# An attention and MoE kernel: dummy matmuls moved to another PSUM bank, six more hidden blocks split into high and low parts, and a scheduler's priorities shifted in 21 stretches

## The chip, the cores and the metric

The kernel runs on one core of one Trainium2 chip. The metric is the device time of one execution in microseconds (us), the median of three runs. Engines are called as in the profile: PE is TensorE, PEld its weight loads, DVE is VectorE, ACT is ScalarE, POOL is GpSimd, SP is SyncE, which issues most DMAs.

## What is computed

Three layers follow each other on 4 batches of 1088 tokens. The attention has 4 heads of 32; its features are products of two projections with 8 columns each.

```python
def phi(x):
    a = einsum('rd,bhsd->bhsr', S1, x)
    b = einsum('rd,bhsd->bhsr', S2, x)
    return einsum('bhsi,bhsj->bhsij', a, b).reshape(*x.shape[:-1], r * r)
kv, z = einsum('bhsf,bhsd->bhfd', phi(k), v), phi(k).sum(axis=2)
x = einsum('bhsf,bhfd->bhsd', phi(q), kv) / (einsum('bhsf,bhf->bhs', phi(q), z)[..., None] + 1e-6)

# x goes on as [4, 1088, 128]
x_prev = x shifted by one token
xk = mu_k * x + (1 - mu_k) * x_prev
xr = mu_r * x + (1 - mu_r) * x_prev
k = maximum(xk @ w_k, 0)                      # 1024 hidden columns
x = sigmoid(xr @ w_r) * ((k * k) @ w_v)

h = maximum(x @ w_in, 0)                      # 1024 columns, halves u and v
v_n = (v - mean(v)) / sqrt(var(v) + 1e-6)
v_s = einsum('ts,bsd->btd', w_spatial, v_n) + b_spatial[None, :, None]
out = (u * v_s) @ w_out
```

## The kernel before

Tokens of a batch are cut into chunks of 384, 384 and 320 (CH), so there are 12 chunks. The hidden columns are cut into blocks of 128: 8 blocks a chunk, 96 blocks in all, numbered g.

Most f32 matmuls are made from fp32r parts: mm3 (line 402) adds three products, low times high, high times high and high times low; the high part is a rounded copy made by ACT (line 405), the low part a subtraction (low, line 408) on DVE or POOL. Each block g goes up (up: three matmuls, relu on ACT at line 679), is squared (sqsplit), and goes down 4 blocks later (down). The letters of PAT say how a block is squared: 'D' squares on ACT (line 700) and goes down as one plain f32 matmul (line 724, two rows of the profile); 'S' multiplies on DVE (line 688), copies the high part on ACT, takes the low part on DVE, and goes down by mm3; 'Q' is as 'S', but its square lies in SBUF and its low part is taken on POOL. G1 and G2 say from which g each pattern holds: the third pattern from g = 26 to 71.

Weights arrive as 64-bit words. split64 (lines 415 to 425) turns them into a high and a low part by five steps on DVE, two or three on ACT, and for 512 columns a product on POOL (line 423). In the start these conversions share DVE with the attention of the first chunks: features (line 521) makes the 64 products per head, k_sum sums keys with values, k_blocks (line 551) masks the sum, q_turn transposes the query features (line 573, into banks 6 and 7) and ACT copies them out, q_num multiplies (line 481) and divides (lines 595 to 597), q_out transposes back (line 611), prep mixes two tokens (lines 617, 636 and 639) and splits the result. Matmuls of a "visit" use half of the array (64 by 64 tiles, line 481) and are kept together.

Dummy matmuls on zeros stand at the start (10 at line 1160) and wherever PE has nothing else to do (keep_busy, line 497, first 8 and then 40); all write bank 7.

No order is written out by hand. The program is recorded first, and arrange then places every instruction: it keeps a planned time for each engine, and among the instructions that could start soon it takes the one with the lowest rank, which is its place in the recorded program. Dummies have a rank behind everything. The result is fixed: each engine runs its list in that order. depend tells arrange which instruction waits for which.

Of the kernel before, what the change touches and what calls it, by code (L numbers as in the profile page):

```python
# [35 lines left out]
IW = 256  # L36
# [18 lines left out]
V2 = 3  # L55
PAT = ('D', 'SD', 'SD', 'S', 'S')
UT = 'x0'
# [34 lines left out]
MARGIN = (30000, 2500)  # L92
IDLE = (8, 40)
SOON = 100
SLACK = {"PE": 60, "Activation": 150, "DVE": 150, "Pool": 200, "SP": 0}
RATES = ((3300, 200), (5000, 300), (8000, 280), (10600, 215), (24000, 350), (float("inf"), 340))
# [103 lines left out]
def depend(todo):  # L200
# [3 lines left out]
    for k, i in enumerate(todo):  # L204
        w, e = {}, engine_name(i)
        for t, (lo, hi, m), write in accesses(i):
# [12 lines left out]
            if t.name.startswith("p"):  # L219
                for k2, lo2, hi2, *_ in seen[name]:  # L220
                    e2 = engine_name(todo[k2])
                    if k2 != k and (e == e2 == "PE" or e != e2 and lo < hi2 and lo2 < hi):
                        w[k2] = w.get(k2, False) or e != e2
# [9 lines left out]
def arrange(tc, after, chain, idle, soon):  # L233
# [33 lines left out]
    lanes = []  # L267
    rank = list(range(len(todo)))
    for k in reversed(range(len(todo))):
# [86 lines left out]
def attn_moe_gmlp(ctx: ExitStack, tc: tile.TileContext, qT, kT, va, st, wk, wv, wr, win, wout,  # L356
# [14 lines left out]
    def bank(i):  # L371
        uid[0] += 1
        return pp.tile([128, 512], F32, tag=f"p{i}", bufs=1, name=f"p{i}_{uid[0]}")
# [120 lines left out]
    def keep_busy(n):  # L494
        w = bank(7)[:, :IW]
        for x in range(n):
            idle.add(TE.matmul(w, lhsT=zero[:, :128], rhs=zero, start=x == 0, stop=x == n - 1).ins.name)  # L497
# [63 lines left out]

    def q_feat(i, wide):
        qp = qst[i] = sb("n1L", [128, 3, 256])
        return features(q_s[i // 3], i % 3, qp, wide, GE if i in QP else None)
# [15 lines left out]

    def q_num(i):
        b, c = divmod(i, 3)
        qt, kb = qst[i], kbd[b]
        nd = bank(5)[:, :396].rearrange("p (t h c) -> p t h c", t=3, h=NH)
        for t in range(3):
# [426 lines left out]
    def group(b, p):  # L1012
# [114 lines left out]
        if last_group:  # L1127
            while gout:
                flush()
            ob = sb(rot(m(6), m(7)), [128, CMAX])  # L1130
            for h in range(2):
                cs = slice(CMAX // 2 * h, CMAX // 2 * h + CMAX // 2)
                tt(VE, u2[:, cs], Z[:, cs], u2[:, cs], ALU.add)
                VE.scalar_tensor_tensor(out=u2[:, cs], in0=pu[:, cs], scalar=0.0, in1=u2[:, cs], op0=ALU.max, op1=ALU.mult)
                TE.matmul(po[1][:, cs], lhsT=wo_last, rhs=u2[:, cs], start=False, stop=h == 1)
            copy(ob, po[1])
            nc.sync.dma_start(out=out[:, b * S + CMAX:b * S + 2 * CMAX], in_=ob)
        else:
            flush()
            pu = pre(d, 1)  # L1140
            gated_out(pu, join(Z, u2), d, 1)
# [15 lines left out]
    VE.memset(zero.bitcast(F32), 0.0)  # L1157
    wp = bank(7)[:, :IW]
    for n in range(NWARM):
# [89 lines left out]

    NI = B * NCH  # L1250
    def meet(sums, num, feat, key):
        wide = bank(4) if (sums, feat, key) != (None,) * 3 else None
        steps = []
        if sums is not None:
            steps.append((k_sums, sums, wide[:, 384:]))
        if num is not None:
            steps.append((q_num, num))
        if feat is not None:
            steps.append((q_feat, feat, wide[:, :192]))
        if key is not None:  # L1260
            steps.append((k_feat, *key, wide[:, 192:384]))
        visit(*steps)

    for g, *what in MEET:
        plan(g, gated(meet) if g < 3 else meet, *what)
    FQ = {f: g for g, _, _, f, _ in MEET if f}
    for j in range(1, NI):
        num = next(g for g, _, n, _, _ in MEET if n == j)
        e = num + OUT
# [206 lines left out]
```

## Time and profile before

| | |
|---|---|
| median of three runs | 438.68 us (438.68 to 438.85) |
| profiled execution | 438.73 us |
| its span, first to last instruction | 436.5 us |
| PE busy | 430.1 us, 3169 matmuls |
| DVE busy | 312.7 us |
| ACT busy | 269.8 us |
| POOL busy | 178.7 us |
| granted PE clock, share of full | 1.00 |

The profile comes from one execution on the chip. Times in its rows count from the start of the span; the execution lasts 2.23 us longer than the span. The start of a row is the start of its first instruction, and PE's rows overlap, because matmuls are pipelined: how fast PE goes is read from one row's start to the next.

### The profile page before, as it was taken

The page shows a single profiled execution, that of the slowest core. Times are in us where ns is not written, and L with a number is a line of the kernel's source. Part 1 is how long each engine was busy: PE and PEld are TensorE (multiplying, and loading weights), DVE is VectorE, ACT ScalarE, POOL GpSimd, SP SyncE. Part 2 cuts the span into 40 slices and gives each one's busy share as a digit, 9 for nine tenths or more (in the row PEclk, how much of TensorE's full clock was granted, in tenths as well). Part 3 has the DMA queues.
Part 4 walks back from the last instruction along what each step waited for, and adds up shares of the span by engine and source line. Part 5 has one row for each costly group of instructions (what it writes and reads, how often), then busy time and mean ns, then how long its engine had stood idle before and what let it go on. Part 6 is the DMA issues. An engine that isn't in the chain of part 4 may idle for free.

```text
span 436.5 us, 8536 instructions
## 1 busy us (share of the span) xinstructions
PE 430.1 (99%) x3169; PEld 402.2 (92%) x3169; DVE 312.7 (72%) x596; ACT 269.8 (62%) x631; POOL 178.7 (41%) x222
## 2 busy tenths in 40 slices
PE   8999999999999999999999999999999999999996
PEld 7968898888888999999999999999999999999995
DVE  5899999889988998684569987834757834525314
ACT  2797999998988987653447654434544434443331
POOL 4153456534345622513321466545346625334220
PEclk9999999999999999999999999999999999999999
DMA  7965010121011111322365223222113222100001
GB/s 228 365 210 177 0 54 20 37 56 47 2 47 32 34 36 38 112 82 73 112 216 176 63 75 119 76 72 65 60 50 119 74 73 65 61 9 16 2 2 50
DMA packets 31385, 34.98 MB, mean 80 GB/s; under 512 B 2864, under 2 KB 26864, under 8 KB 31344
## 3 DMA queue, kind: packets, MB, share of 16 engines
q1 hardware_dynamic: 31056, 34.36, 25.0%
q8 instruction: 25, 0.41, 0.4%
q14 instruction: 16, 0.13, 0.1%
q10 hardware_dynamic: 288, 0.08, 0.1%
HBM read 25.91 MB, written 8.52 MB: 79 GB/s over the span
## 4 chain that ended last, share of the span: by engine, by line
PE 82%; DVE 11%; ACT 3%; POOL 2%; issue 1%; POOLq 0%; DVEq 0%; ACTq 0%
PE p L402 63%; PE p L481 6%; PE p L724 6%; DVE VR L822 3%; PE p L573 2%; DVE bn L816 1%; DVE m L939 1%; PE p L1040 1%; PE p L1039 1%; DVE m L408 1%; POOL rs L819 1%; PE p L611 1%; PE p L497 1%; DVE VR L939 1%; PE p L1160 1%
## 5 line engine op out<-in xcount | busy, mean ns | idle before, releaser
L402 PE MATMUL p<-m,k 128*128 128x384 f32 (+1 forms) x288 | 69.5, 357 | 0.3 <-DVE w L408 0.2
L402 PE MATMUL p<-w,k 128*128 128x384 f32 (+1 forms) x360 | 63.4, 323 | 0.0
L402 PEld LDWEIGHTS p<-w,k 128*128 128x128 f32 x360 | 58.9, 188 | 0.7
L939 DVE TENSOR_TENSOR m<-p,m 128x384 f32<-128x384 f32 (+2 forms) x37 | 19.2, 518 | 55.5 <-PE p L1040 54.9
L402 PEld LDWEIGHTS p<-m,k 128*128 128x128 f32 x288 | 48.0, 188 | 9.1 <-DVE w L408 2.2
L405 ACT ACTIVATE m<-m 128x384 fp32r<-128x384 f32 (+2 forms) x46 | 23.3, 506 | 46.1 <-DVE m L1053 35.4
L408 POOL TENSOR_TENSOR k<-VR,k 128x512 fp32r<-128x512 f32 x25 | 33.0, 1319 | 41.1 <-ACT k L405 36.7
L679 ACT ACTIVATE m<-p 128x384 f32<-128x384 f32 (+1 forms) x96 | 44.8, 473 | 4.1 <-PE p L402 3.6
L405 ACT ACTIVATE m<-p 128x384 f32<-128x384 f32 (+2 forms) x44 | 20.8, 476 | 33.4 <-PE p L402 24.9
L408 DVE TENSOR_TENSOR m<-m,m 128x384 fp32r<-128x384 f32 (+1 forms) x44 | 30.7, 697 | 11.0 <-ACT m L405 10.4
L402 PE MATMUL p<-w,n1H 128*128 128x384 f32 (+1 forms) x192 | 37.5, 325 | 0.0
L402 PE MATMUL p<-w,n1L 128*128 128x384 f32 (+1 forms) x168 | 33.1, 323 | 0.0
L408 POOL TENSOR_TENSOR w<-st,w 128x384 fp32r<-128x384 f32 (+1 forms) x15 | 14.9, 995 | 43.5 <-ACT w L405 43.4
L688 DVE TENSOR_TENSOR p<-p,m 128x384 f32<-128x384 f32 (+1 forms) x56 | 29.6, 533 | 4.0 <-ACT m L679 3.4
L402 PEld LDWEIGHTS p<-w,n1H 128*128 128x128 f32 x192 | 32.0, 188 | 0.4
L822 DVE TENSOR_SCALAR VR<-VR,mv,rs 128x512 f32<-128x512 f32 x24 | 22.0, 915 | 12.6 <-POOL rs L819 12.5
L405 ACT ACTIVATE k<-VR 128x512 fp32r<-128x512 f32 x25 | 15.8, 631 | 21.4 <-PE p L402 16.5
L402 PEld LDWEIGHTS p<-w,n1L 128*128 128x128 f32 x168 | 28.2, 188 | 0.3
L724 PE MATMUL p<-w,wvT 128*128 128x384 f32 (+1 forms) x72 | 28.0, 470 | 0.0
L818 POOL TENSOR_SCALAR rs<-mv 128x1 f32<-128x1 f32 x34 | 9.6, 282 | 44.9 <-DVE mv L817 44.2
L408 DVE TENSOR_TENSOR w<-p,w 128x384 fp32r<-128x384 f32 (+1 forms) x48 | 25.2, 532 | 1.9 <-ACT w L405 1.5
L408 POOL TENSOR_TENSOR n1H<-VR,n1H 128x512 fp32r<-128x512 f32 x12 | 16.5, 1373 | 23.8 <-ACT n1H L405 23.6
(279 smaller groups left out, 1147.0 us busy)
## 6 DMA issues: line engine op xcount, KB each, us to landing
vd<-VR SPq DMA_DIRECT2D x24, 256.0 KB, 2.0
VR<-vd SPq DMA_DIRECT2D x24, 256.0 KB, 2.8
st<-in_wT_dram SPq DMA_DIRECT2D x16, 192.0 KB, 2.4
w<-in_kT_dram SPq DMA_DIRECT2D x8, 192.0 KB, 4.5
w<-in_qT_dram SPq DMA_DIRECT2D x8, 192.0 KB, 3.5
VR<-in_wT_dram SPq DMA_DIRECT2D x8, 192.0 KB, 2.4
out_dram<-m SPq DMA_DIRECT2D x8, 192.0 KB, 1.9
m<-in_wT_dram SPq DMA_DIRECT2D x8, 192.0 KB, 3.0
```

Of the source, the lines that this page charges most:

```text
L402: TE.matmul(out_ap, lhsT=l, rhs=r, start=first and n == 0, stop=last and n == 2, skip_group_check=skip)
L405: return SE.activation(out=dst, in_=src, func=AF.Copy)
L408: return eng.tensor_tensor(out=L, in0=src, in1=H.bitcast(F32), op=ALU.subtract)
L481: ins = TE.matmul(out_ap, lhsT=l, rhs=r, start=start, stop=stop)
L497: idle.add(TE.matmul(w, lhsT=zero[:, :128], rhs=zero, start=x == 0, stop=x == n - 1).ins.name)
L573: TE.transpose(pt[:, cut(c, t)], qp[:, t, 128 * g:128 * g + 128], idn)
L679: SE.activation(out=r, in_=hk, func=AF.Relu)
L688: anchor[0] = VE.tensor_tensor(out=sq, in0=hk, in1=r, op=ALU.mult)
L724: TE.matmul(vvs[i], lhsT=(wvT if f % 2 else wvE)[:, f // 2], rhs=hls.pop(g), start=f == 0, stop=f == NF - 1)
L818: GE.tensor_scalar(out=rs, in0=mv[:, 1:2], scalar1=1e-6, scalar2=None, op0=ALU.add)
L822: VE.tensor_scalar(out=v, in0=r, scalar1=mv[:, 0:1], scalar2=rs, op0=ALU.subtract, op1=ALU.mult)
L939: return eng.tensor_tensor(out=o, in0=a, in1=b_, op=op)
```

## The change

The dummies write bank 3 instead of bank 7, and the first series has 6 instead of 8. Bank 3 is next used by the first down product. In the third pattern every eighth block is 'Q' instead of 'D': g = 31, 39, 47, 55, 63 and 71, of which 47 and 71 have 320 columns. For the last output tile the two parts of 192 columns become 256 and 128, and its last copy is made half by ACT and half by DVE. depend now keeps the recorded order of instructions of one engine that touch the same PSUM tile, for every engine and not for PE alone. In 21 stretches of the recorded program (WOBBLE: seed, size, first and last place) a fixed pseudo-random number is added to the rank. meet can now take several query tiles in one visit; the list MEET is the same, so that each visit has one as before.

```diff
-PAT = ('D', 'SD', 'SD', 'S', 'S')
+PAT = ('D', 'SD', 'SDSDSDSQ', 'S', 'S')
...
-IDLE = (8, 40)
+IDLE = (6, 40)
 SOON = 100
+WOBBLE = ((18397, 200, 21, 41), (9184, 10, 58, 208), (56298, 10, 61, 81), (39075, 30, 70, 220), (47392, 80,
...
             if t.name.startswith("p"):
                 for k2, lo2, hi2, *_ in seen[name]:
                     e2 = engine_name(todo[k2])
-                    if k2 != k and (e == e2 == "PE" or e != e2 and lo < hi2 and lo2 < hi):
+                    if k2 != k and (e == e2 or lo < hi2 and lo2 < hi):
                         w[k2] = w.get(k2, False) or e != e2
...
-    rank = list(range(len(todo)))
+    rank = [float(k) for k in range(len(todo))]
+    for seed, size, lo, hi in WOBBLE:
+        for k in range(lo, min(hi, len(todo))):
+            rank[k] += size * ((k * k * 7 + k * 40503 + seed * 25173) % 65521 / 65521 - .5)
...
     def keep_busy(n):
-        w = bank(7)[:, :IW]
+        w = bank(3)[:, :IW]
...
-            for h in range(2):
-                cs = slice(CMAX // 2 * h, CMAX // 2 * h + CMAX // 2)
+            for h, cs in enumerate((slice(0, 256), slice(256, CMAX))):
                 tt(VE, u2[:, cs], Z[:, cs], u2[:, cs], ALU.add)
                 VE.scalar_tensor_tensor(out=u2[:, cs], in0=pu[:, cs], scalar=0.0, in1=u2[:, cs], op0=ALU.max, op1=ALU.mult)
                 TE.matmul(po[1][:, cs], lhsT=wo_last, rhs=u2[:, cs], start=False, stop=h == 1)
-            copy(ob, po[1])
+            copy(ob[:, :CMAX // 2], po[1][:, :CMAX // 2])
+            VE.tensor_copy(ob[:, CMAX // 2:], po[1][:, CMAX // 2:])
...
-    wp = bank(7)[:, :IW]
+    wp = bank(3)[:, :IW]
     for n in range(NWARM):
         TE.matmul(wp, lhsT=zero[:, :128], rhs=zero, start=n == 0, stop=n == NWARM - 1)
```

How the lists change is shown at three places. A row reads: line, operation, written tile, read tiles, shape, count; the first number in a tile's name is its place (p7 is bank 7, w12 a weight slot), the rest tells uses of that place apart. Lines of the changed kernel are 8 higher from keep_busy on.

PE at the first key sum (tiles n0H, n0L, n1H, into p5), the transposes of the first query tile (n1L, into p6 and p7), the dummies (x3) and the first product with the masked sum kb0, before:

```order
L481 MATMUL p5_55_215<-xs0H_35_147,n0H_44_172 64x33 x12
L481 MATMUL p5_55_215<-xs0H_35_147,n0L_47_183 64x33 x11
L573 MATMUL p6_56_228<-idn_2_64,n1L_50_194 128x128 x3
L481 MATMUL p5_55_215<-xs0H_35_147,n0L_47_183 64x33
L497 MATMUL p7_28_106<-x3_26_93 128x256 x2
L573 MATMUL p7_57_233<-idn_2_64,n1L_50_194 128x128 x3
L481 MATMUL p5_55_215<-xs0H_35_147,n1H_53_205 64x33 x8
L481 MATMUL p5_55_215<-va0_36_151,n1H_53_205 64x33 x4
L497 MATMUL p7_58_238<-x3_26_93 128x256 x4
L481 MATMUL p5_60_305<-kb0_59_303,VR_1_63 64x66 x12
```

and now, in the changed kernel:

```order
L489 MATMUL p5_55_213<-xs0H_35_145,n0H_44_170 64x33 x12
L489 MATMUL p5_55_213<-xs0H_35_145,n0L_47_181 64x33 x12
L505 MATMUL p3_58_236<-x3_26_93 128x256
L581 MATMUL p7_57_231<-idn_2_64,n1L_50_192 128x128 x3
L581 MATMUL p6_56_226<-idn_2_64,n1L_50_192 128x128 x3
L489 MATMUL p5_55_213<-xs0H_35_145,n1H_53_203 64x33 x8
L489 MATMUL p5_55_213<-va0_36_149,n1H_53_203 64x33 x4
L505 MATMUL p3_58_236<-x3_26_93 128x256 x4
L489 MATMUL p5_60_303<-kb0_59_301,VR_1_63 64x66 x12
```

The key sum is no longer cut by transposes, the six transposes stand together, and one dummy stands there instead of two.

DVE a little later: the last step of the third wk chunk's conversion (w9), the five steps of the first wv chunk's (w12, w13, read from w8), and the products of the second visit (n1L of the query, n0H of the next batch's key), before:

```order
L420 TENSOR_SCALAR w9_74_362<-w9_74_362 128x512
L415 TENSOR_SCALAR w12_78_379<-w8_70_348 128x512
L417 TENSOR_SCALAR w13_79_380<-w8_70_348 128x512
L418 SCALAR_TENSOR_TENSOR w13_79_380<-w8_70_348,w13_79_380 128x512
L419 SCALAR_TENSOR_TENSOR w12_78_379<-w8_70_348,w12_78_379 128x512
L420 TENSOR_SCALAR w12_78_379<-w12_78_379 128x512
L521 TENSOR_TENSOR n1L_85_399<-p4_84_398,bs1_86_406 128x768
L521 TENSOR_TENSOR n0H_87_407<-p4_84_398,bs0_88_414 128x768
```

and now:

```order
L428 TENSOR_SCALAR w9_74_360<-w9_74_360 128x512
L433 SCALAR_TENSOR_TENSOR k1_11_78<-w16_72_349,w15_71_348 128x256
L529 TENSOR_TENSOR n1L_85_397<-p4_84_396,bs1_86_404 128x768
L423 TENSOR_SCALAR w12_78_377<-w8_70_346 128x512
L425 TENSOR_SCALAR w13_79_378<-w8_70_346 128x512
L426 SCALAR_TENSOR_TENSOR w13_79_378<-w8_70_346,w13_79_378 128x512
L427 SCALAR_TENSOR_TENSOR w12_78_377<-w8_70_346,w12_78_377 128x512
L428 TENSOR_SCALAR w12_78_377<-w12_78_377 128x512
L529 TENSOR_TENSOR n0H_87_405<-p4_84_396,bs0_88_412 128x768
```

The product n1L has moved ahead of the five steps; the low half of the second wk chunk (k1), which was made before line 408 of the first chunk of x, now stands behind line 420.

PE around the visit that uses the second query tile (kb0 with VR, then Sbd with w1 and w2), the last two up blocks of the first chunk (m11, m13 into p0 and p1) and the first down matmuls (line 724, into p3), before:

```order
L573 MATMUL p7_93_432<-idn_2_64,n1L_85_399 128x128 x3
L402 MATMUL p1_138_599<-m11_66_333,k1_11_78 128x384
L402 MATMUL p1_138_599<-m11_66_333,k0_10_77 128x384
L402 MATMUL p1_138_599<-m13_67_334,k0_10_77 128x384
L724 MATMUL p3_113_518<-w4_91_425,x2_15_82 128x384
L481 MATMUL p5_100_459<-kb0_59_303,VR_1_63 64x66 x12
L481 MATMUL p4_99_458<-Sbd_33_130,w1_34_145 64x64 x6
L481 MATMUL p4_99_458<-Sbd_33_130,w2_40_163 64x64 x6
L724 MATMUL p3_113_518<-w5_98_456,wvT_14_81 128x384
L724 MATMUL p3_113_518<-w6_108_502,x2_15_82 128x384
L724 MATMUL p3_113_518<-w7_114_520,wvT_14_81 128x384
L611 MATMUL p5_115_522<-idn_2_64,VR_1_63 128x128 x3
```

and now (the transposes p7 stand some rows further up):

```order
L505 MATMUL p3_58_236<-x3_26_93 128x256 x6
L489 MATMUL p5_100_457<-kb0_59_301,VR_1_63 64x66 x12
L489 MATMUL p4_99_456<-Sbd_33_128,w1_34_143 64x64 x6
L489 MATMUL p4_99_456<-Sbd_33_128,w2_40_161 64x64 x6
L732 MATMUL p3_113_516<-w4_91_423,x2_15_82 128x384
L732 MATMUL p3_113_516<-w5_98_454,wvT_14_81 128x384
L410 MATMUL p0_127_560<-m11_66_331,k1_11_78 128x384
L410 MATMUL p0_127_560<-m11_66_331,k0_10_77 128x384
L410 MATMUL p0_127_560<-m13_67_332,k0_10_77 128x384
L732 MATMUL p3_113_516<-w6_108_500,x2_15_82 128x384
```

The visit now comes ahead of two up blocks and of all down matmuls; the six dummies in front of it are the last ones, since the first down matmul needs their bank.

## Rows read from the trace of the kernel before

**Rows 1.** The page, busy time of PE with its share and instructions

```profile
PE 430.1 (99%) x3169; PEld 402.2 (92%) x3169; DVE 312.7 (72%) x596; ACT 269.8 (62%) x631; POOL 178.7 (41%) x222
```

**Rows 2.** Waits of PE: total us, times, longest us

```profile
PE p L1160 <- DVE half L1163: 1.2, 1, 1.2
PE p L573 <- DVE n1L L521: 0.9, 1, 0.9
```

**Rows 3.** Busy us of each engine by stretch, with granted clock, DMA share, GB/s

```profile
12.00:20.00 8.00, 7.93 (x89) 7.15 (x90) 7.45 (x20) 5.00 (x13) 0.00 (x0) 1.00 1.03 383
20.00:30.00 10.00, 9.13 (x89) 7.05 (x88) 9.79 (x17) 9.90 (x24) 5.32 (x6) 1.00 0.68 226
...
60.00:120.00 60.00, 60.00 (x623) 52.30 (x622) 53.82 (x110) 55.96 (x145) 28.59 (x32) 1.00 0.11 30
120.00:230.00 110.00, 109.80 (x674) 103.35 (x673) 84.64 (x173) 75.24 (x183) 40.06 (x57) 1.00 0.26 79
...
272.00:430.00 158.00, 157.77 (x941) 155.69 (x942) 82.12 (x140) 66.19 (x136) 65.09 (x68) 1.00 0.17 54
```

**Rows 4.** Timeline of PE in the start: start us, us, instruction, idle before

```profile
10.00 0.50 PE L497 MATMUL p<-x 128*128 128x256 f32 x2
10.56 0.55 PE L573 MATMUL p<-idn,n1L 128*128 128x128 f32 x3
11.03 0.66 PE L481 MATMUL p<-xs0H,n1H 128*64 128x33 f32 x16
...
17.11 1.91 PE L402 MATMUL p<-m,k 128*128 128x384 f32 x9
...
21.72 2.03 PE L402 MATMUL p<-m,k 128*128 128x384 f32 x9
...
26.83 0.92 PE L481 MATMUL p<-kb,VR 128*64 128x66 f32 x24
...
30.42 0.49 PE L611 MATMUL p<-idn,VR 128*128 128x128 f32 x3
```

**Rows 5.** Timeline of DVE in the start

```profile
11.97 0.30 DVE L551 TENSOR_TENSOR kb<-p,mk 128x132 f32<-128x132 f32 x1 [1.41 <-PE p L481]
...
15.89 0.62 DVE L639 SCALAR_TENSOR_TENSOR mx<-p,mus,m 128x384 f32<-128x384 f32 x1 [0.18 <-ACT m L617]
...
19.69 0.43 DVE L420 TENSOR_SCALAR w<-w 128x512 int32<-128x512 int32 x1
...
20.36 1.55 DVE L417 TENSOR_SCALAR w<-w 128x512 int32<-128x512 int32 x1
...
23.62 0.95 DVE L521 TENSOR_TENSOR n1L<-p,bs 128x768 f32<-128x768 f32 x1
```

**Rows 6.** Timeline of POOL in the start

```profile
20.27 1.36 POOL L423 TENSOR_TENSOR k<-w,w 128x512 fp32r<-128x512 f32 x1 [9.65 <-DVE w L420]
```

**Rows 7.** The chain that ended last, in order of time: start us, us, what

```profile
72.62 0.65 PE p L724 x2
73.27 1.04 PE p L402 x6
...
98.25 0.54 PE p L724 x2
98.79 0.87 PE p L402 x6
```

**Rows 8.** The page, groups of instructions: busy us, mean ns, idle before

```profile
L688 DVE TENSOR_TENSOR p<-p,m 128x384 f32<-128x384 f32 (+1 forms) x56 | 29.6, 533 | 4.0 <-ACT m L679 3.4
...
L408 POOL TENSOR_TENSOR w<-st,w 128x384 fp32r<-128x384 f32 (+1 forms) x15 | 14.9, 995 | 43.5 <-ACT w L405 43.4
```

**Rows 9.** Timeline of all engines in the tail

```profile
430.97 0.36 DVE L939 TENSOR_TENSOR m<-p,m 128x192 f32<-128x192 f32 x1
...
432.01 0.36 DVE L1134 SCALAR_TENSOR_TENSOR m<-p,m 128x192 f32<-128x192 f32 x1
...
433.10 0.49 ACT L405 ACTIVATE m<-p 128x384 f32<-128x384 f32 x1 [0.60 <-PE p L1135]
```

More of the change, by code (lines that the diff above doesn't have):

```diff
@@ L560, in k_sums, with q_feat @@
         return (), lambda: k_blocks(b, kv)
-    def q_feat(i, wide):
-        qp = qst[i] = sb("n1L", [128, 3, 256])
+    def q_feat(i, wide, tag="n1L"):
+        qp = qst[i] = sb(tag, [128, 3, 256])
         return features(q_s[i // 3], i % 3, qp, wide, GE if i in QP else None)
@@ L579, in attn_moe_gmlp, with q_num @@
     nd_pe, nd_last, x_turn, first_x = [None], [None], [None], []
-    def q_num(i):
+    def q_num(i, at=5):
         b, c = divmod(i, 3)
         qt, kb = qst[i], kbd[b]
-        nd = bank(5)[:, :396].rearrange("p (t h c) -> p t h c", t=3, h=NH)
+        nd = bank(at)[:, :396].rearrange("p (t h c) -> p t h c", t=3, h=NH)
         for t in range(3):
@@ L1250, in attn_moe_gmlp, with each @@
     NI = B * NCH
+    def each(x):
+        return x if isinstance(x, tuple) else () if x is None else (x,)
     def meet(sums, num, feat, key):
@@ L1255, in meet @@
             steps.append((k_sums, sums, wide[:, 384:]))
[L1256 to L1259, printed above, removed]
+        for n, j in enumerate(each(num)):
+            steps.append((q_num, j, 5 - n))
+        for n, j in enumerate(each(feat)):
+            steps.append((q_feat, j, wide[:, 192 * n:192 * n + 192], ("n1L", "n1H")[n]))
         if key is not None:
@@ L1265, in attn_moe_gmlp @@
         plan(g, gated(meet) if g < 3 else meet, *what)
-    FQ = {f: g for g, _, _, f, _ in MEET if f}
+    FQ = {j: g for g, _, _, f, _ in MEET for j in each(f)}
     for j in range(1, NI):
-        num = next(g for g, _, n, _, _ in MEET if n == j)
+        num = next(g for g, _, n, _, _ in MEET if j in each(n))
         e = num + OUT
```

4 rows, old and new, of the table WOBBLE are left out of this document.

## The prediction

> **What bounds the kernel now.** I read the page's busy times first: TensorE (PE) is busy for 430.1 us of 436.5 [rows 1]. Busy is not the same as limited, so the second view is PE's own waits: only two are longer than 0.2 us, 1.2 us before the first instruction and 0.9 us in front of the transposes of line 573 [rows 2]. The third is the table by stretch [rows 3]. In 20 to 30 us PE is busy 9.13 of 10 us and VectorE (DVE) 9.79; in 60 to 120 us PE is full and DVE has 53.82 of 60; in 272 to 430 us PE is full but for 0.23 us and DVE is half idle. The reader is to see two regimes. Up to about 25 us a chain runs through DVE, and PE fills its holes with dummies (line 497). From there on PE always has the next matmul at hand, so the span is the moment at which PE becomes full, plus the sum of PE's work, plus the last few microseconds when everything waits for one output. A gain must come from one of these three; moving rows that PE never waits for is worth nothing.
>
> **The start: the dummies' own bank.** Before, the last two of the first eight dummies share bank 7 with the second half of the transposes of q, so these stand behind them: dummies at 10.00, transposes at 10.56, the last part of the key sum at 11.03 [rows 4]. In the changed order one dummy is left there and the six transposes follow each other. Three transposes and the change of tile size behind them take 0.47 us (10.56 to 11.03), the two dummies 0.56 us. I let the one dummy cost half of that, 0.28, and drop one change of tile size with the split key sum: the last part starts 0.7 to 0.8 us earlier. DVE waits for exactly that in row 11.97, with 1.41 us of idle time ahead [rows 5], so the whole chain to the first x moves by about 0.75 us: line 639 could start at 15.1 instead of 15.89.
>
> Part of it is spent at once: between the division (line 597) and line 639 five conversion steps stand instead of four, three of them 512 wide instead of none. The eight rows from line 639 at 15.89 to line 420 at 19.69 take 3.80 us, 0.475 each [rows 5]; the fifth row costs about that, so I put line 639 at 15.5 and, with two conversions' copies now ahead of the copy of x on ScalarE, the first up matmul at 17.2, against 17.11 [rows 4]. Its bounds are 16.4 (all of the 0.75 kept) and 17.9.
>
> What was moved ahead comes back directly behind. Line 420 of the third wk chunk stood eight rows after line 639, now five. With 0.475 us a row it starts at 17.9 instead of 19.69, and GpSimd (POOL) can build the low half of that chunk (20.27 to 21.63 before, [rows 6]) from 18.3 on. PE's fifth up block, which waited for it at 21.72, can go from 19.7 on. The product n1L (line 521) of the next query tile stood behind all five steps of the next conversion, at 23.62; now it stands ahead of them, two rows behind line 420, at about 18.8. The wait of 0.9 us in front of line 573 [rows 2] is that product, so it goes. One of the five steps was line 417 at 20.36 with 1.55 us, and it starts 0.09 us after POOL's row of 1.36 us and ends 0.28 after it, 1.1 us later than a row of 0.475 would. In the new order n1L, which reads PSUM, stands beside POOL's row, so the five steps shrink from 3.5 us (20.12 to 23.62) to about 2.4. They end near 22.3, and the second product of that visit follows them.
>
> The visit on PE (lines 481, 26.83 before) needs both copies of the turned q tile; ScalarE makes the second of them behind a conversion's copy, which needs the fourth of the five steps (done near 21.9). Two copies of half a microsecond each, as the one at 433.10 [rows 9], put the visit at 22.9. That is 3.9 us earlier, but with six up matmuls (0.173 us each, [rows 7]) and one f32 pair (0.65) less done before it: 1.7 us of work has moved behind it. Net 2.2 us. Until line 611 (30.42 before) both orders have the same work to do, which gives 28.2 there.
>
> What is late next: the second conversion's sums on POOL and line 408 of the second chunk of x, which now stands behind one more product of 0.95 us. I take 0.3 us off for that. **The start is worth -1.9 us**, with -0.8 (only the 0.75 of the first step survives) and -2.5 (nothing is taken off, first up matmul at 16.9) as its ends.
>
> One load goes against it. The values of the next batch (528 KB) now pass the queries and keys of the second chunk on SP's queue. At 383 GB/s [rows 3] that makes those 1.4 us later. Their first reader is the visit right after the first x; the new order puts twelve dummies ahead of it: 256 columns each, at 0.173 us for 384 [rows 7] 0.115 us, together 1.4 us too. So it is hidden, barely; if not, it costs a few tenths, which is inside the range.
>
> **Six blocks split.** Six of the 96 hidden blocks change from one f32 matmul to three fp32r ones. The f32 pair of rows takes 0.65 us at 384 columns and 0.54 at 320; three fp32r matmuls take 0.52 (1.04 for six) and 0.435 (0.87 for six) [rows 7]. Four blocks of 384 and two of 320: 4 x 0.13 + 2 x 0.105 = 0.73 us less on PE, where nothing hides it. The price is one DVE product of 0.53 us and one POOL subtraction of about 1.0 us per block [rows 8]; ScalarE makes a copy where it made a square. Together 3.2 us of DVE in a stretch that has 6.2 us free [rows 3], and 6 us of POOL, which has half its time free. I take **-0.7 us**; the bad end is in the third rival.
>
> Row 20.36 [rows 5] shows what a POOL row beside a DVE row can cost: 1.1 us. The Trainium skill (SBUF — State Buffer, "SBUF: two separate sides") says that DVE and GpSimd share a pair of ports as an exclusive lock for a whole instruction, taken also by a DVE operation with two SBUF inputs. By that rule each of the six new subtractions can hold a DVE step for up to its own length, about 6 us in all; row 20.36 agrees with it. The sum above goes without it, because row 20.36 shows only one step caught by one POOL row, and most DVE rows of that stretch read PSUM.
>
> **The tail.** The last product now goes in 256 and 128 columns instead of twice 192, and the last copy is halved between ScalarE and DVE. Four DVE steps from 430.97 to 432.37 [rows 9] have the same columns in sum, 1.40 us again. The last f32 matmul has a third less columns: between 432.37 and the copy at 433.10 lie 0.73 us, of which I give it 0.1. The copy of 0.49 us becomes two halves; a 192-wide DVE step takes 0.36, so 0.13 to 0.2 are saved. **-0.25 us** (0 to -0.35).
>
> **Everything else that moved.** From 30 to 320 us rows change places on every engine; behind that, PE's order is the old one up to the tail. PE's idle time there is small before (none in 60 to 120, 0.2 us in 120 to 230, [rows 3]), so there is little to win and each new wait is a loss. I take 0, with -0.5 and +0.7.
>
> **The sum.** The profiled execution took 438.73 us, 2.23 more than its span of 436.5; the median of the three timed runs, 438.68, is the same within 0.05. 436.5 - 1.9 - 0.7 - 0.25 = 433.65, and with 2.23 around it **435.9 us**.
>
> **Rivals.** *First: the lead is given back.* DVE is busy 9.79 of 10 us at 20 to 30 and 53.82 of 60 later. If DVE gets less far ahead than PE, PE catches up with it and waits. For it: DVE's work is not less, only better packed. Against it: after 30 us PE did not wait for DVE, so there is a store of finished work between them. Then only a quarter of the start's gain stays: 438.73 - 0.45 - 0.7 - 0.25 = 437.3.
>
> *Second: the change does nothing that can be measured.* The new order is made for planned durations; on the chip the first up matmul comes at 17.9 and the later holes just move, the split blocks lose on DVE what they save on PE, and the tail's two copies wait for the same matmul. Then 438.5.
>
> *Third: slower, by DVE between 60 and 120 us.* The six products (3.2 us) and one caught DVE step per subtraction (6 x 1.1 = 6.6 us) make 9.8 us of new DVE time against 6.2 us free: 3.6 us overflow. PE has no other work then, so it waits. With the start's lead kept this is 438.73 - 1.9 - 0.25 - 0.7 + 3.6 = 439.5; with a quarter of it, 440.9. Slower by what can be measured needs the given-back lead and five of the six subtractions to catch a step (3.2 + 5 x 1.1 - 6.2 = 2.5 us against 1.4 gained). Against it: 3.2 of the 9.8 are sure, the rest needs a hit each time.
>
> **How the numbers follow.** Forecast (435.0 to 436.9) 0.58; lead given back (436.9 to 437.8) 0.22; no change 0.12; slower 0.08, which I place between 439.6 and 441. A measurement of this kernel can tell 0.2%, 0.88 us, from no change: faster means below 437.8, slower above 439.6. That makes 0.80 faster, 0.12 same, 0.08 slower. The low end of the range adds the good ends, -2.5 - 0.75 - 0.35 - 0.5, to 434.6; the high end takes in the lead given back and a third of the no-change case, 438.0, and about 0.17 is left out above it.
>
> **What would show it.** The product of the key mask (line 551) near 11.2 instead of 11.97; n1L near 18.8; no wait at line 573; line 611 of the second query tile near 28.2 instead of 30.42; the lead of about 2 us still there at 60 us. In the table by stretch PE stays full between 60 and 120 us with DVE near 57 of 60. In the tail the time from line 1135 to the last copy's end falls by 0.25. Wrong would be: the first up matmul after 17.9, a DVE wait of PE in the blocks that were split, or a PE wait on a load at 15 to 17 us.

## The result, and the profile after

The changed kernel takes 434.99 us, the median of 5 runs (434.49 to 435.35), against 438.73 us for the kernel before in the same session (438.68 to 438.85): a ratio of 0.9912, with a 95% interval of 0.9901 to 0.9923. The prediction was 435.9 us, with 434.6 to 438.0 as its range. The profiled execution is the fastest of the five, 434.49 us; its span is 432.7 us, 3.8 less than before. The other four have spans of 433.1 to 433.6 us.

The page of the profile after, busy time and instructions (it answers to [rows 1]):

```profile
PE 426.8 (99%) x3173; PEld 401.8 (93%) x3173; DVE 311.5 (72%) x603; ACT 269.6 (62%) x631; POOL 185.9 (43%) x228
```

PE's waits after, total us, times, longest us (they answer to [rows 2]; lines are 8 higher):

```profile
PE p L1168 <- DVE ebias L1170: 1.2, 1, 1.2
PE p L489 <- ACT VR L413: 0.4, 1, 0.4
```

Busy us by stretch, with the columns of [rows 3], and stretches set some 4 us earlier where the work runs that much earlier:

```profile
56.00:116.00 60.00, 60.00 (x633) 53.49 (x632) 55.41 (x112) 56.65 (x145) 32.76 (x37) 1.00 0.12 34
116.00:226.00 110.00, 109.83 (x676) 103.33 (x675) 86.69 (x176) 77.04 (x186) 44.21 (x60) 1.00 0.25 77
```

The 0.9 us in front of the transposes are gone, and a wait of 0.4 us for ACT's copy of a turned query tile has come; two more waits are of 0.2 us each. PE is still full from 56 to 116 us, although DVE has 55.41 of 60 instead of 53.82. PE's and DVE's start, as in [rows 4] and [rows 5]:

```profile
9.03 0.82 PE L581 MATMUL p<-idn,n1L 128*128 128x128 f32 x6
9.78 0.66 PE L489 MATMUL p<-xs0H,n1H 128*64 128x33 f32 x16
...
16.71 1.29 PE L410 MATMUL p<-m,k 128*128 128x384 f32 x6
...
22.23 0.92 PE L489 MATMUL p<-kb,VR 128*64 128x66 f32 x24 [0.42 <-ACT VR L413]
...
27.90 0.49 PE L619 MATMUL p<-idn,VR 128*128 128x128 f32 x3
```

```profile
10.72 0.30 DVE L559 TENSOR_TENSOR kb<-p,mk 128x132 f32<-128x132 f32 x1 [0.44 <-PE p L489]
...
17.92 0.95 DVE L529 TENSOR_TENSOR n1L<-p,bs 128x768 f32<-128x768 f32 x1
...
19.39 0.41 DVE L425 TENSOR_SCALAR w<-w 128x512 int32<-128x512 int32 x1
```

Row 27.90 stood at 30.42, so the lead is 2.52 us there. The mask product is 1.25 earlier, the product n1L 5.7, and the step that took 1.55 us beside POOL takes 0.41. At the last step of a chunk (line 736, DVE; 728 before) the lead is some 2.8 us from 70 to 96 and 3.1 to 3.4 from 123 to 161; single rows that have changed places lie above or below that. From 313 us on, where both orders are the same again, it is 3.88 up to the tail. The last part of it is lost again in the tail (all engines, as in [rows 9]):

```profile
427.06 0.42 DVE L947 TENSOR_TENSOR m<-p,m 128x256 f32<-128x256 f32 x1
...
428.17 0.29 DVE L1141 SCALAR_TENSOR_TENSOR m<-p,m 128x128 f32<-128x128 f32 x1
...
429.09 0.33 ACT L413 ACTIVATE m<-p 128x192 f32<-128x192 f32 x1 [0.49 <-PE p L1142]
429.45 0.36 DVE L1144 COPY m<-p 128x192 f32<-128x192 f32 x1 [0.99 <-ACT m L413]
429.84 0.33 SPq L1145 DMA_DIRECT2D out_dram<-m  x1
```

DVE's half copy starts when ACT's has ended, and its wait is one for ACT: the two halves stand behind each other. That wait is in the program: both copies read one PSUM bank (p5), and DVE's instruction waits for ACT's semaphore. From the first of the four steps to the output's DMA it is 2.78 us, where before it was 2.65, from 430.97 [rows 9] to this row:

```profile
433.62 0.33 SPq L1137 DMA_DIRECT2D out_dram<-m  x1
```

### The profile page after: what moved, and what is told of

It reads as the page before. It is cut to its first block, busy times and chain, and to the rows that moved or that the text cites. A ratio compares the mean times of both kernels' runs of the same rounds, so it can differ in the third digit from the quotient of the medians.

```text
span 432.7 us, 8563 instructions
## 1 busy us (share of the span) xinstructions
PE 426.8 (99%) x3173; PEld 401.8 (93%) x3173; DVE 311.5 (72%) x603; ACT 269.6 (62%) x631; POOL 185.9 (43%) x228
## 4 chain that ended last, share of the span: by engine, by line
PE 88%; DVE 4%; ACT 2%; DMA 2%; SPq 1%; POOL 1%; issue 1%; POOLq 0%; ACTq 0%; DVEq 0%
PE p L410 73%; PE p L732 5%; PE p L489 5%; PE p L1048 1%; PE p L581 1%; PE p L1047 1%; DVE VR L830 1%; DMA va<-in_va_dram 1%; DMA xs0H<-in_va_dram 1%; PE p L619 1%; SPq L465 1%; DVE bn L824 1%; PE p L895 0%; PE p L894 0%; POOL rs L827 0%
## 5 line engine op out<-in xcount | busy, mean ns | idle before, releaser
L410 PE MATMUL p<-m,k 128*128 128x384 f32 (+1 forms) x288 | 66.4, 348 | 0.2 <-ACT m L687 0.2
L410 PE MATMUL p<-w,k 128*128 128x384 f32 (+1 forms) x360 | 65.3, 324 | 0.0
L947 DVE TENSOR_TENSOR m<-p,m 128x384 f32<-128x384 f32 (+3 forms) x37 | 19.2, 520 | 55.6 <-PE p L1048 55.1
L410 PE MATMUL p<-w,n1H 128*128 128x384 f32 (+1 forms) x192 | 39.6, 325 | 0.0
L413 ACT ACTIVATE m<-p 128x384 f32<-128x384 f32 (+3 forms) x44 | 20.5, 470 | 29.2 <-PE p L410 21.3
L416 DVE TENSOR_TENSOR m<-m,m 128x384 fp32r<-128x384 f32 (+1 forms) x44 | 29.5, 673 | 10.9 <-ACT m L413 10.2
L410 PE MATMUL p<-w,xs1H 128*128 128x384 f32 (+1 forms) x108 | 28.3, 331 | 0.0
L830 DVE TENSOR_SCALAR VR<-VR,mv,rs 128x512 f32<-128x512 f32 x24 | 20.1, 838 | 8.6 <-POOL rs L827 8.6
```

Of the source, the lines that this page charges most:

```text
L410: TE.matmul(out_ap, lhsT=l, rhs=r, start=first and n == 0, stop=last and n == 2, skip_group_check=skip)
L413: return SE.activation(out=dst, in_=src, func=AF.Copy)
L416: return eng.tensor_tensor(out=L, in0=src, in1=H.bitcast(F32), op=ALU.subtract)
L830: VE.tensor_scalar(out=v, in0=r, scalar1=mv[:, 0:1], scalar2=rs, op0=ALU.subtract, op1=ALU.mult)
L947: return eng.tensor_tensor(out=o, in0=a, in1=b_, op=op)
```

## Experiments

My theory was the prediction's: the start is worth 1.9 us, most of it through the dummies' own bank, the six split blocks 0.7, and what moves later nothing. The first rival says that the order, not the bank, makes the gain. The second says that the shifts behind the start have a share of their own. All times are medians; all ratios are to the kernel before in the same session (438.79 to 438.85 us). A difference below about 0.4 us between two kernels is within the intervals.

### The bank, the shifts and the tail

*Dummies back in bank 7, six of them in the first series, all else changed:*

```diff
 def keep_busy(n):
-    w = bank(3)[:, :IW]
+    w = bank(7)[:, :IW]
...
-    wp = bank(3)[:, :IW]
+    wp = bank(7)[:, :IW]
```

> The changed kernel with its dummies back in bank 7; all else, the 6 instead of 8 first dummies too, stays. Theory of the prediction (the own bank frees the first transposes): the first key sum is late again, the mask product near 11.5 instead of 10.72 us, and the time about 0.7 us above the changed kernel, 435.7. Rival (6 instead of 8 dummies did that, since none is left over at the transposes): the mask product stays within 0.1 us of where it is at the same clock, and the time changes by the later visit alone, whose second transposes now wait for the last dummy: 435.0 to 435.4.

Measured: 438.46 us, ratio 0.9993 (0.9984 to 1.0002), far above both forecasts of the time. The mask product came at 11.07, so the first key sum was not late although the bank was the old one (11.20 in bank 3, in the kernel with the old tail below): in this order no dummy is left among the transposes. The bank decides later. PE, dummies (x), second transposes and the visit behind them:

```profile
22.41 0.28 PE L505 MATMUL p<-x 128*128 128x256 f32 x1
22.75 0.55 PE L581 MATMUL p<-idn,n1L 128*128 128x128 f32 x3
23.88 0.92 PE L489 MATMUL p<-kb,VR 128*64 128x66 f32 x24 [0.58 <-ACT VR L413]
```

The second half of the second query tile's transposes has to stand behind the dummies of its bank, and the visit comes 1.65 us after row 22.23 above. Line 619 follows at 28.66 (27.90), which is only 0.76 later, and about 0.5 of that is the early part of the profiled run (last section); the remaining loss, some 3 us, comes between 30 and 90 us, where arrange made another order too. So the run shows that bank and shifts belong together, not what the bank is worth alone.

*No shifts, all else changed:*

```diff
-WOBBLE = ((18397, 200, 21, 41), (9184, 10, 58, 208), ...
+WOBBLE = ()
```

> The changed kernel with an empty list of shifts. Theory: the first 0.7 us of the start stay, but the product n1L of the second query tile stands behind a whole conversion again, so line 611 of that tile comes near 29.7 instead of 27.90 us, and the time is 436.5 to 437.0. Rival (the shifts only move work that PE never waits for): 435.0 within 0.3.

Measured: 438.93 us, ratio 1.0006 (0.9997 to 1.0015), about 2 us above my forecast. Line 615, where the changed kernel has 27.90:

```profile
29.51 0.49 PE L615 MATMUL p<-idn,VR 128*128 128x128 f32 x3
```

Without the shifts nothing of the change can be measured: bank, shorter series, split blocks and tail cancel out.

*Only the nine shifts that end by place 262:*

```diff
-WOBBLE = ((18397, 200, 21, 41), ... (38805, 30, 2294, 3294))
+WOBBLE = ((18397, 200, 21, 41), ... (36869, 30, 228, 248))
```

> The changed kernel with the nine shifts that end at place 262 or before; the other twelve are taken out. Theory: the start is the same, line 611 of the second query tile near 27.9 us, and only the tenths won after 140 us are lost: 435.2 to 435.6. Rival (the lead of the start is kept only because the later shifts make room for it): over 436.3, with the lead shrinking between 40 and 150 us.

Measured: 437.58 us, ratio 0.9974 (0.9966 to 0.9983). The start is the changed one, but 2.6 us are missing at the end. I had expected nearly all of the gain here, and the second rival is right. Line 615, and the longest of PE's new waits, which the kernel without shifts has too:

```profile
28.40 0.49 PE L615 MATMUL p<-idn,VR 128*128 128x128 f32 x3
...
PE p L406 <- DVE w L412: 1.0, 1, 1.0
```

*The old tail in the changed kernel* (two parts of 192, one copy on ACT):

> The changed kernel with the last product in 192 and 192 columns and one copy by ScalarE, as before. Theory of the prediction (the tail is worth 0.25 us): 435.25. Rival (the two half copies stand one behind the other, the second waits for the first): the time from the first addition of the last product to the last DMA's issue falls from 2.78 to 2.65 us, and the kernel is 0.1 us faster, 434.9.

Measured: 434.79 us, ratio 0.9909 (0.9895 to 0.9923): the rival, though 0.2 us can't be told from no difference. Its trace lies 0.45 us behind that of the changed kernel at the first of the last four DVE steps (427.51 and 427.06) and 0.33 behind at the last DMA (430.17 and 429.84): the new tail costs 0.12 to 0.13 us.

### The tail's parts, the split blocks and the bank each alone

*The new parts of 256 and 128, but one whole copy on ACT:*

```diff
-            copy(ob[:, :CMAX // 2], po[1][:, :CMAX // 2])
-            VE.tensor_copy(ob[:, CMAX // 2:], po[1][:, CMAX // 2:])
+            copy(ob, po[1])
```

> The changed kernel with its last product in 256 and 128 columns, but the last copy whole, on ScalarE. Theory (the two half copies stand behind each other, 0.33 and 0.36 us, because the second waits for the first; the narrower last matmul is worth the 0.1 us that the prediction gave it): the stretch from the first of the last four VectorE steps to the output's DMA falls from 2.78 us to about 2.55, and the time is 434.6 to 434.8. Rival (the narrower last matmul is what costs, for instance since its two parts are no longer equal on VectorE): it stays at 2.65 or above, and the time is that of the kernel with the old tail or of the changed kernel, 434.8 to 435.0.

Measured: 434.77 us, ratio 0.9905 (0.9892 to 0.9919). All engines in its tail:

```profile
427.65 0.42 DVE L947 TENSOR_TENSOR m<-p,m 128x256 f32<-128x256 f32 x1
...
429.69 0.49 ACT L413 ACTIVATE m<-p 128x384 f32<-128x384 f32 x1 [0.49 <-PE p L1142]
430.20 0.33 SPq L1144 DMA_DIRECT2D out_dram<-m  x1
```

From the first step to the DMA it is 2.55 us: the narrower last matmul gives 0.10, as predicted, and the halved copy takes 0.23. This is the lowest median of the study, but it can't be told from that of the changed kernel or of the one with the old tail.

*The changed kernel without the split blocks:*

```diff
-PAT = ('D', 'SD', 'SDSDSDSQ', 'S', 'S')
+PAT = ('D', 'SD', 'SD', 'S', 'S')
```

> The changed kernel with its third pattern as before, so that the six blocks are again squared on ScalarE and go down as f32 pairs. Theory (the split blocks give 0.73 us of TensorE time, and VectorE, 55.4 of 60 us busy from 56 to 116 us, hides their price): 435.7, with the shifts applied to a program that is a few instructions shorter behind the first such block. Rival one (the price on VectorE and GpSimd eats the gain): 435.0 or below. Rival two (the shifts fit one program only, and every later place is moved by the missing instructions): the loss is as large as with the later shifts left out, 437 and above, with TensorE gaps of some tenths of a us spread over 60 to 140 us.

Measured: 438.77 us, ratio 0.9997 (0.9988 to 1.0006), the second rival. The last step of a chunk (line 736, DVE) shows what the first two blocks do, first in the changed kernel, then in this one:

```profile
67.31 0.49 DVE L736 TENSOR_TENSOR x<-p,m 128x320 f32<-128x320 f32 x1
...
93.78 0.55 DVE L736 TENSOR_TENSOR x<-p,m 128x384 f32<-128x384 f32 x1
```

```profile
67.91 0.49 DVE L736 TENSOR_TENSOR x<-p,m 128x320 f32<-128x320 f32 x1
...
94.65 0.54 DVE L736 TENSOR_TENSOR x<-p,m 128x384 f32<-128x384 f32 x1
```

The distance is 0.60 us ahead of the first split block and 0.87 behind the second: 0.27 for two blocks of 384, where the prediction has 2 x 0.13. From 313 us on it stays at 4.1 us, far more than six blocks. A block that isn't split has one DVE, one POOL and two PE instructions less, so every later shift falls on other instructions than in the changed kernel. The loss between is in many pieces; the longest wait of PE behind the start is 0.4 us.

*The kernel before with the six blocks split, nothing else* (the third pattern of PAT):

> The kernel before with the six blocks split, nothing else. Theory (as predicted, 0.73 us less on TensorE, nothing given back): 438.1, and TensorE without waits of its own from 60 to 120 us. Rival (with the old priorities the six new steps on VectorE and six on GpSimd come late, and TensorE waits): 438.7 to 439.5, with waits in the blocks from 75 us on.

Measured: 439.73 us, ratio 1.0019 (1.0010 to 1.0027): slower, and above both forecasts. The denominator of a query tile (line 595, DVE), two visits in the kernel before, then the same two in this one:

```profile
125.87 0.15 DVE L595 TENSOR_SCALAR de<-p 128x12 f32<-128x12 f32 x1
134.36 0.16 DVE L595 TENSOR_SCALAR de<-p 128x12 f32<-128x12 f32 x1
```

```profile
125.17 0.16 DVE L595 TENSOR_SCALAR de<-p 128x12 f32<-128x12 f32 x1
135.66 0.17 DVE L595 TENSOR_SCALAR de<-p 128x12 f32<-128x12 f32 x1
```

At 125 us this kernel is 0.70 us ahead and ten us later 1.30 behind. The 0.70 is not the price of the blocks: one visit earlier the two kernels are level (118.81 and 118.82), and PE's line 611 at 128.89 is 0.36 ahead, since the order of the rows has changed as well. Four of the six blocks had been split by then, which [rows 7] puts at 0.50. The 1.3 us stay from 160 us to the tail. In between, PE, DVE and POOL of this kernel:

```profile
130.85 0.55 PE L573 MATMUL p<-idn,n1L 128*128 128x128 f32 x3 [0.33 <-DVE tt L822]
...
133.71 0.70 PE L402 MATMUL p<-m,k 128*128 128x320 f32 x3 [1.00 <-DVE w L408]
```

```profile
131.64 1.54 DVE L408 TENSOR_TENSOR m<-mx,m 128x384 fp32r<-128x384 f32 x1
133.11 0.54 DVE L408 TENSOR_TENSOR w<-p,w 128x384 fp32r<-128x384 f32 x1
```

```profile
131.48 1.29 POOL L408 TENSOR_TENSOR n1L<-VR,n1H 128x512 fp32r<-128x512 f32 x1 [1.53 <-PE p L573]
```

The subtraction of mx starts 0.16 us after POOL's row and takes 1.54 us. DVE in the kernel before:

```profile
130.81 0.55 DVE L408 TENSOR_TENSOR w<-p,w 128x384 fp32r<-128x384 f32 x1
...
132.66 0.56 DVE L408 TENSOR_TENSOR m<-mx,m 128x384 fp32r<-128x384 f32 x1 [1.17 <-ACT m L405]
```

There the step had to wait for ACT's copy until 132.63, when POOL's row of 1.36 us from 131.29 was at its end, and the low part w had been made ahead of it. Here w stands behind it, and PE waits 1.00 us. PE's waiting row is an up block, which does not read w; in the program's lists it writes the bank (p1) that the step w<-p,w still reads. The Trainium skill ("SBUF — State Buffer", section "SBUF: two separate sides") says that a DVE operation with two SBUF inputs and a GpSimd operation that reads SBUF hold their shared ports by turns for a whole instruction; the row agrees, since both inputs of the caught step lie in SBUF and the extra 1.0 us is close to the 1.13 us that POOL's row still had to run; the step behind it, which reads p in PSUM, takes its usual 0.54 us beside POOL's next row (132.72 to 134.04). In the kernel with nine shifts the same step takes 1.54 us as well, without any shift 1.55, and PE's 1.0 us wait above is the same one.

*The kernel before with the dummies in bank 3 and a first series of six, nothing else:*

> The kernel before with the dummies in bank 3 and six of them in the first series, nothing else. Theory (the order of the start comes from the shifts; the bank and the shorter series only free the first key sum): the mask product near 11.2 us instead of 11.97, but line 611 of the second query tile at 29.5 or later, as without the shifts (29.51), and the time 438.3 to 438.8. Rival (the bank makes the start by itself, and what the changed kernel without shifts lost it lost in the split blocks and the tail): line 611 near 28.4 and the time 437 or below.

Measured: 438.22 us, ratio 0.9989 (0.9980 to 0.9998). The mask product came at 11.13, 0.84 us earlier than before. Line 611, where the kernel before has 30.42:

```profile
29.59 0.49 PE L611 MATMUL p<-idn,VR 128*128 128x128 f32 x3
```

The bank and the shorter series bring 0.83 us at line 611, and of that 0.5 or so is left at the end; which of the two does it is not separated. The theory holds in the numbers but not in its "only": with no shift at all n1L of the second query tile already comes at 19.32 instead of 23.62, and PE's wait of 0.9 us in front of line 573 is gone. A wait of 0.8 us for ACT's copy has come in its place. (The profiled run was 1.0 us above the median, with a PE wait of 0.9 us at 40 us for nothing that the profile shows; the profile without shifts has 0.7 us at the same place. Both lie behind line 611.)

### What a shift is worth

*The six blocks split with their low part on DVE:*

```diff
-PAT = ('D', 'SD', 'SDSDSDSQ', 'S', 'S')
+PAT = ('D', 'SD', 'SDSDSDSS', 'S', 'S')
```

> The changed kernel with 'S' instead of 'Q' for the six blocks: they are split all the same, but their square lies in PSUM and their low part is taken on VectorE, not on GpSimd, so that the recorded program has the same instructions at the same places and the shifts fall on the same ones. Theory (GpSimd takes work off VectorE, which has 55.4 of 60 us in that stretch; six more steps of about 0.5 us make 58.7): 435.3 to 437, with VectorE waits of TensorE between 75 and 120 us. Rival (the six GpSimd subtractions hold VectorE's steps up, as the row of 1.55 us beside a GpSimd row did before): 434.8 or below.

Measured: 436.82 us, ratio 0.9953 (0.9941 to 0.9965), inside the theory's range. So POOL is the better place in this order. But the VectorE waits that I expected of PE are not there: its longest new wait is 0.3 us for a POOL product, and PE is idle for 0.36 of 60 us from 56 to 116. The rest of the 1.4 us that it falls behind between 76 and 185 us is spread over many small pieces, and I can't name one cause.

*The twelve later shifts with other seeds, each raised by one:*

> The changed kernel with the seeds of the twelve later shifts each raised by one: same stretches, same sizes, same start, other patterns. Theory (a shift is worth something only as a pattern that was found for this one program; another one is as good as none): near the kernel with the nine early shifts alone, 436.5 to 438.5. Rival (it is the loosening of the order in these stretches that helps, whatever the pattern): 434.6 to 435.6.

Measured: 438.83 us, ratio 0.9998 (0.9989 to 1.0006), 1.25 us worse than without these twelve and above the theory's range. PE's new waits, of which the second lies at 7 us, ahead of all twelve shifts (last section):

```profile
PE p L410 <- ACT m L676: 0.8, 1, 0.8
...
PE p L489 <- DMA xs0H<-in_va_dram: 0.4, 1, 0.4
```

*The first fourteen shifts, up to place 1070:*

> The changed kernel with its first fourteen shifts, up to place 1070 of the program; TensorE's order is the changed one up to 104 us. The kernel with nine shifts lost some 0.4 us by 67 us, 1.15 by 120 and 2.4 by 245. Theory (the loss grows step by step, and each group of shifts takes its own part of it): 436.0 to 436.8, with the loss beginning behind 110 us. Rival one (the shifts up to 1070 carry all of it): 434.9 to 435.4. Rival two (the whole is one tuned chain, and any cut loses as much as another): 437 or above.

Measured: 436.57 us, ratio 0.9944 (0.9931 to 0.9956), as the theory said. The trace runs beside that of the changed kernel (0.1 us behind) up to 94 us, is 0.5 behind at 135 and 1.6 from 310 us on.

*The twelve later shifts alone:*

> The changed kernel with the twelve later shifts alone, the nine early ones left out, so that the start is the one without shifts (line 615 of the second query tile at 29.5 us, against 27.9 in the changed kernel). Theory (the early shifts are worth the start's 1.1 to 1.6 us, the later ones 2.4 us, and both add): 436.4 to 437.0. Rival (the later patterns fit only what the early ones leave): 438.5 to 440, as without any shift.

Measured: 436.41 us, ratio 0.9941 (0.9929 to 0.9953), as the theory said. The transposes of x (PE, lines 619 and 615), first in the changed kernel, whose row at 27.90 stands above, then in this one:

```profile
49.41 0.49 PE L619 MATMUL p<-idn,VR 128*128 128x128 f32 x3
...
131.92 0.49 PE L619 MATMUL p<-idn,VR 128*128 128x128 f32 x3
```

```profile
29.62 0.49 PE L615 MATMUL p<-idn,VR 128*128 128x128 f32 x3
...
51.14 0.49 PE L615 MATMUL p<-idn,VR 128*128 128x128 f32 x3
...
133.68 0.49 PE L615 MATMUL p<-idn,VR 128*128 128x128 f32 x3
```

The distance is 1.72, 1.73 and 1.76 us (some 0.5 of it is the early part of the profiled run, last section); at the last four DVE steps it is 1.98. What the start loses is carried through 400 us of full PE, neither caught up nor grown by more than 0.3. With the shifts the times add up: none 438.93, the nine early ones alone 437.58 (-1.35), the twelve later ones alone 436.41 (-2.52), both 434.99 (-3.94, where the sum is -3.87).

## Why the prediction was right, and where it was not

**The three regimes hold.** PE was full from 30 us on, and the lead of the start was still there at the end. The twelve later shifts alone show this best, with a distance that stays for 400 us. The first rival, a lead given back, is out.

**The start, -1.9, was right in size.** At line 611 it is 2.52, of which about 0.5 belongs to the profiled run and not to the kernel (last section); 2.0 is left. The intermediate times are near. In the profiled run and in the kernel with the old tail, which has the same start, the mask product comes at 10.72 and 11.20 (11.2 forecast), n1L at 17.92 and 18.41 (18.8), the first up product at 16.71 and 17.20 (17.2), the visit at 22.23 and 22.71 (22.9), line 611 at 27.90 and 28.38 (28.2), and there is no wait at line 573. The caught step of 1.55 us is gone, as said. **The reason was half wrong.** I wrote "the dummies' own bank", but the first key sum is freed in bank 7 as well when the series has six. The bank and the series bring 0.83 us at line 611, near the 0.75 that the prediction gave the first step; the nine shifts bring the other 1.1 (29.51 to 28.40). Their worth at the end, 1.35 us, is about this much. They are not what moves n1L ahead of the conversion: that happens without them, and they bring it from 19.23 to 18.40 and the visit's wait for ACT's copy from 0.8 to 0.4 us.

**The six blocks, -0.7, were right on PE and wrong as a whole.** PE gains as worked out where it can be read: 0.27 us for two blocks. The failed step is the price at which I put the collisions in that term: nothing. Alone in the old order the blocks make the kernel 0.9 us slower. It is the mechanism of the third rival, one DVE step of 1.54 us caught beside POOL, a POOL row that had been there before. But it came at 131 us and not between 60 and 120, where DVE had room for the six products, and it took one hit in front of a step that PE waits for instead of five. (Row 20.36, which the prediction takes as agreeing with the rule for two SBUF inputs, reads one tile, w; row 131.64 is the case with two.) In the changed kernel the same step is caught too, and PE does not notice. DVE, POOL and PE:

```profile
127.65 0.56 DVE L416 TENSOR_TENSOR w<-p,w 128x384 fp32r<-128x384 f32 x1
...
128.59 1.41 DVE L416 TENSOR_TENSOR m<-mx,m 128x384 fp32r<-128x384 f32 x1
```

```profile
128.29 1.29 POOL L416 TENSOR_TENSOR n1L<-VR,n1H 128x512 fp32r<-128x512 f32 x1 [1.58 <-PE p L581]
```

```profile
129.05 0.92 PE L489 MATMUL p<-kb,VR 128*64 128x66 f32 x24
129.90 0.50 PE L410 MATMUL p<-winH,w 128*128 128x512 f32 x1
130.24 0.60 PE L410 MATMUL p<-m,k 128*128 128x320 f32 x3
```

The visit of 0.85 us stands on PE during those 1.41 us, and the low part w, by the programs' lists the same one, had been made ahead of the caught step, at 127.65, where in the slower order it stood behind.

**Everything else, 0, was the mis-sized term.** Against the kernel before, the lead grows by another 0.65 us behind the start beside the 0.73 of the blocks (from 2.5 to 3.9). Against the same program without them, the later shifts are worth 2.5. I read the small idle time of PE before as "little to win". One thing that the later shifts do is shown: with the blocks split and without these shifts w stands behind the caught step and PE waits 1.0 us, and with them alone or all together w stands ahead and the wait is gone. The kernel with fourteen shifts does not have it either and is 1.0 us faster than the one with nine; the other 1.6 us go with the last seven shifts, in pieces that I can't name. Of the sum's terms, -0.7 for the blocks was too good by more than a microsecond in the old order, and 0 for the rest was too bad by more than that. That they cancelled is luck.

**The tail, -0.25, failed.** The narrower matmul gave its 0.10, but the two half copies do not run beside each other. The prediction named this case in its second rival (though by another cause) and left it out of the term's bounds, which ended at 0; measured is +0.13 for the tail as a whole.

In all, the span of the median run fell by 3.3 us, from 436.5 to 433.2: 2.0 in the start, 0.73 in the blocks by their price, 0.65 in the rest, less 0.13 in the tail. The profiled run adds its 0.5 us of the early part. **The time around the span was a term that the prediction kept and should not have.** It carried 2.23 us over from the kernel before; in the five runs of the changed kernel it is 1.75 to 1.82, so 0.43 of the 3.74 us were won outside the span. The forecast of the span, 433.65, was off by 0.45 us, and that of the time by 0.9, half of it from here.

What stays open: what the bank is worth within the changed order, since moving it back moves other instructions too; which of the later shifts avoids which wait; what shortens the time around the span; and what the new rule in depend does, which was not tried alone.

## What to carry to other kernels

When one engine is always full, a lead won at the start stays to the end, and a saved microsecond on that engine counts only if no new wait comes with it: look for the DVE steps with two SBUF inputs that will now meet a GpSimd row, and for what PE waits for right behind them, an operand or a bank. An order set by pseudo-random shifts is worth its gain for one program only: with other seeds, the split blocks left out or the bank moved back the 3.7 us were gone but for 0.4 at most, with the low parts on another engine half of them were, so such a search belongs at the end of the work and has to be repeated after each edit. Two engines that each copy half of a tile can stand behind each other, here by a wait in the program; look for it before counting on half the time. And a change can move the time around the span: compare spans as well as times.

## What the runs showed of the hardware

PE's matmuls double their rate some microseconds into the span, and the moment differs between profiled runs with the same start. PE's and other engines' busy us in the sixth microsecond, before and after:

```profile
5.00:6.00 1.00, 1.00 (x14) 0.78 (x15) 0.00 (x0) 0.00 (x0) 0.00 (x0) 1.00 0.92 237
```

```profile
5.00:6.00 1.00, 1.00 (x28) 0.87 (x29) 0.00 (x0) 0.18 (x1) 0.00 (x0) 1.00 0.96 298
```

PE was busy with the same dummies and visit products in both (their tiles are 128 by 64, as the form 128*64 in PE's rows has it, not 64 by 64). It did 14 matmuls in that microsecond before and 28 after, the factor between its levels of 1.2 and 2.4 GHz, while the column of the granted clock prints 1.00; in the kernel before, the distance of the products halves only at 7.0 us. In two kernels with the changed kernel's start (the old tail, the one copy) this microsecond still has 14, and their traces lie 0.48 us behind from 13 us on. The other four runs of the changed kernel have spans of 433.1 to 433.6 us, against 432.7. The kernel with fourteen shifts has 25 in that microsecond of its profiled run, which is its fastest, 436.09 us against a median of 436.57. But an early rise alone does not bring the 0.5 us: the kernels without split blocks and with other seeds have 22 and 21, and there PE then waits 0.7 and 0.4 us for a load at 7 us, and line 619 comes at 28.48 and 28.33. That the early rise makes the 0.5 us where the loads are in time fits, but was not tested.

The time of an execution around its span belongs to the program. It was 2.17 to 2.34 us in all 71 executions of the kernel before beside the experiments and 2.19 to 2.29 in the eleven with only the bank and the series changed, but 1.73 to 2.00 in all runs of the other twelve kernels. So the blocks split alone, with 1.74 to 1.83, lose more in the span than in the time: 437.9 us against 436.6, in the medians. What in the program makes it is not shown.
